# Gated memory attention with a GEGLU layer on one core: a third buffer for projected pairs, and the last chunk's side work put elsewhere

## The chip, the core and the metric

The kernel runs on one core of a Trainium2 chip. A core has five engines that work side by side: TensorE (matrix products), VectorE, ScalarE, GpSimd, and SyncE, which issues the transfers (DMAs). The metric is the device time of one launch in microseconds, the median of several runs.

## What is computed

The input x has 2,048 rows of 576 numbers. Two branches work on it, and a gate for each row mixes their results. Cut to what matters:

```python
g = sigmoid((x * gate_w).sum(-1, keepdims=True))
a = attention_with_memory(x, wq, wk, wv, wo, beta)
b = (gelu(x @ w_gate) * (x @ w_up)) @ w_down          # 576 -> 4608 -> 576
return g * a + (1 - g) * b

# attention_with_memory: 32 heads of 18 columns, 4 chunks of 512 rows
for s in range(4):
    qs, ks, vs = q[:, :, s], k[:, :, s], v[:, :, s]
    a_dot = softmax(qs @ ks.T * scale + mask) @ vs     # within the chunk
    a_mem = (phi(qs) @ M) / (phi(qs) @ z + 1e-6)       # from the chunks before
    outs.append(sigmoid(beta) * a_mem + (1 - sigmoid(beta)) * a_dot)
    M = M + phi(ks).T @ vs
    z = z + phi(ks).sum(over rows)
# phi(t) = t + 1 where t > 0, else exp(t)
```

## The kernel before, in words

**Pairs.** Numbers are kept as pairs of float16 tiles, a high word and a low word: ScalarE rounds to the high word, VectorE or GpSimd subtracts it from the float32 value to get the low word. Products take both words and add up in float32.

**Projections.** x is worked off in four chunks `s` of 512 rows. In a chunk after the first, TensorE begins with four row blocks `q`. Each makes the values of its 128 rows in two halves (`vrows`, L307 to L310, in the two banks `dn`), which VectorE turns into pairs (`put_rows`, `vstage`, L488) and a DMA stores. A half needs the bank that the vstage of an earlier half frees. Beside them stand the memory steps of the chunk before: `key_rows` (L548 to L551), `memorize` (L563) and `recall` (L520). Then come nine projections `j`, one for each column block of the queries and keys (`project`, L297 and L300). `put_columns` turns the result of one into a pair: ScalarE writes the high word (L453) into a tile `stage` and an exponential `expm` (L458), VectorE the low word (L465) and its part of phi (L463), GpSimd the rest of phi (L464), and SyncE issues the store `qk<-stage`. The tile `stage` has two buffers, so the pair after next waits for the store of this one.

Side work is put by hand into the row blocks (`beside_rows`) and the projections (`beside_products`): loading and splitting the next chunk of x, `rescale(c)` (L165: it brings two chunks to one scale, with one VectorE operation over 4,608 columns, L170), the sums of the parts of x that the later layer wants (`form_sums`: a subtraction L344, a high word on ScalarE L345, a low word on VectorE; `last_sum`: a subtraction on GpSimd L352 and words, the low word at L355), and for the first weights of that layer the sums of squares (`squares`, L80), the scales (`scales`, `scales_out`), their application on GpSimd (`scale_g`, L247) and their splitting into pairs (`high_g` on ScalarE, `low_g` on GpSimd L278, `sums_g` on GpSimd L267 to L270).

**The later layer and the attention.** After the fourth chunk a loop of 72 steps `v` runs over 36 blocks `f` of 128 hidden columns and the two halves `p` of the rows; v = 2f + p. A step makes the products of a block of `w_gate` and `w_up` with two chunks at once, seven products of parts and sums of parts in place of eight. They go to three banks, V, X (bank G) and Y (bank U):

```python
V, X, Y = bank("V"), bank("G"), bank("U")
product(V, f, S3, t, 8, 10, True); rest(V, ...)   # first
dve.tensor_copy(g1, V)                            # L1078
product(X, f, A11, x1, 0, 4, True); dve.tensor_copy(Y, X)   # L1082
product(V, f, A22, x2_, 0, 4); rest(V, ...)       # third; waits for L1078
...
product(Y, f, S1, t, 0, 2); dve.tensor_tensor(g1, Y, g1, OP.add)   # L1110
product(Y, f, S4, x2_, 2, 6); rest(Y, ...)        # last; waits for L1110
hidden(f, e, Y, g1)                               # L964, L968, L969
```

The products are at L984 and L991. From step 2 on, the attention of a head stands between them.

**Order.** The instructions of TensorE, VectorE, ScalarE and GpSimd run in the order in which the code issues them. The order on SyncE's queue is set by a scheduler from the whole program. A few operations of `put_columns` are issued later, by `finish_later()`. `zo` is the scale of the result, four lines at the end of the projections (L792 to L795), eight small operations once its helper is counted.

## Time and profile before

| | |
|---|---|
| median of 3 runs | 1689.53 us (1688.03 to 1690.39) |
| the profiled execution, its own time | 1691.98 us |
| its span in the profile | 1690.3 us |
| mean granted TensorE clock in it | 0.993 of full speed |
| busy: TensorE, VectorE, GpSimd, ScalarE | 97%, 75%, 68%, 64% of the span |

The span is what the profile sees of one execution; the rest of its own time lies around it. Times in rows of the profile count from the start of the span. A row of the timeline is start, duration, engine, line and operation, what is written and read, how many instructions (x12), and in brackets the idle time before it with what ended it: `[4.62 <-DVE vstage L488]` is 4.62 us of idleness that ended with VectorE's vstage. A row of waits is engine, tile and line, what it waited for, then the total, the count and the longest. A row of the stretches is start and end, length, TensorE's busy time with its count, the granted clock, the busy share of the DMA engines and the GB/s. A row of groups ends in count, busy time, mean ns and idle time before. Of the chain of waits a row is start, duration, engine and line.

In this profile the first chunk begins within the first 30 us; the row blocks of the second, third and fourth chunk begin near 65, 124 and 187 us, the loop of 72 steps at 254.7 us.

### The profile page before, as it was taken

What the parts mean: (1) busy time and instruction counts of PE and PEld (TensorE: products, weight loads), DVE (VectorE), ACT (ScalarE), POOL (GpSimd) and SP (SyncE); (2) the same over time, 40 slices, a digit from 0 to 9 for tenths busy, and PEclk for the clock granted to TensorE, in tenths of its full rate; (3) what the DMA queues carried; (4) which work ended last, traced back from release to release, by engine and by line L of the source; (5) the groups of instructions that cost most, each with busy time, mean ns of one, the idle gap of its engine ahead of it and who ended that gap; (6) DMA issues with size and microseconds to landing.
All of it is one profiled execution on the core that took longest, in us unless ns stands there. A gap on an engine that the chain in (4) does not pass through costs nothing.

```text
span 1690.3 us, 31950 instructions
## 1 busy us (share of the span) xinstructions
PE 1638.8 (97%) x11884; PEld 987.6 (58%) x11884; DVE 1266.0 (75%) x3154; ACT 1083.6 (64%) x1770; POOL 1146.5 (68%) x1057
## 2 busy tenths in 40 slices
PE   8899898899999999999999999999999999999999
PEld 4556654455655556655556555565555555565577
DVE  5556686688788888888788777888887887876543
ACT  6565344777767777777777777767777677762200
POOL 2231445887878888887869697887878797875300
PEclk9999999999999999999999999999999999999999
DMA  6522332556666465656566564747466565635351
GB/s 222 193 98 89 127 109 71 113 109 124 119 130 131 104 128 109 124 112 125 113 141 121 114 126 103 143 100 137 110 131 128 117 129 107 131 70 119 85 120 64
DMA packets 462348, 200.54 MB, mean 119 GB/s; under 512 B 421232, under 2 KB 431728, under 8 KB 461680
## 3 DMA queue, kind: packets, MB, share of 16 engines
q1 hardware_dynamic: 462192, 198.50, 52.7%
q8 instruction: 93, 1.52, 0.4%
q14 instruction: 63, 0.52, 0.1%
HBM read 82.60 MB, written 27.26 MB: 65 GB/s over the span
## 4 chain that ended last, share of the span: by engine, by line
PE 68%; DVE 16%; ACT 7%; POOL 4%; issue 3%; DMA 2%; DVEq 0%; ACTq 0%; SPq 0%; POOLq 0%
PE dn L942 17%; PE U L984 13%; PE V L984 7%; PE G L984 7%; PE pv L896 3%; DVE pf L854 3%; PE st L307 3%; PE st L848 3%; PE V L991 2%; DVE acc L950 2%; DVE junk L80 2%; PE dn L307 2%; PE U L991 2%; DMA qk<-stage 1%; POOL hh L969 1%
## 5 line engine op out<-in xcount | busy, mean ns | idle before, releaser
L942 PE MATMUL dn<-paird,hh 128*128 128x288 f16 x3402 | 488.4, 286 | 4.9 <-DVE acc L950 4.0
L984 PEld LDWEIGHTS <-pairg 128*128 128x128 f16 x3024 | 290.6, 98 | 298.2 <-issue 27.6
L877 POOL TENSOR_TENSOR ph<-pf,ph 128x512 f16<-128x512 f32 (+1 forms) x256 | 358.8, 1402 | 96.3 <-ACT ph L876 59.0
L942 PEld LDWEIGHTS <-hh 128*128 128x128 f16 x3456 | 337.1, 98 | 144.2 <-issue 7.9
L950 DVE SCALAR_TENSOR_TENSOR acc<-dn,ev,acc 128x288 f32<-128x288 f32 x535 | 268.0, 512 | 51.1 <-PE dn L942 48.7
L867 ACT ACTIVATE pf<-pf,mb,esc 128x512 f32<-128x512 f32 (+3 forms) x512 | 292.9, 642 | 3.0
L854 DVE CUSTOM_DVE_ANT_0 pf<-st,mask 128x512 f32<-128x512 f32 (+3 forms) x512 | 229.2, 485 | 75.6 <-PE st L848 72.5
L969 POOL TENSOR_TENSOR hh<-gl,hh 128x512 f16<-128x512 f32 x144 | 173.3, 1204 | 141.3 <-ACT hh L968 141.2
L984 PE MATMUL U<-xt,pairg 128*128 128x512 f16 x864 | 211.5, 381 | 4.8 <-DVE gl L1093 3.9
L984 PE MATMUL G<-x,pairg 128*128 128x512 f16 x864 | 210.0, 379 | 0.5 <-DVE stage L465 0.5
L278 POOL TENSOR_TENSOR pairg<-raw,pairg 128x512 f16<-128x512 f32 (+2 forms) x144 | 179.2, 1266 | 36.9 <-ACT pairg L274 36.9
L876 ACT ACTIVATE ph<-pf 128x512 f16<-128x512 f32 (+1 forms) x256 | 184.3, 720 | 0.0
L974 ACT ACTIVATE gl<-gl,sc 128x512 f32<-128x512 f32 x144 | 103.6, 720 | 94.1 <-DVE gl L1110 52.4
L864 ACT ACTIVATE mb<-mx,esc 128x4 f32<-128x4 f32 x128 | 37.4, 292 | 191.0 <-DVE mx L854 190.8
L968 ACT ACTIVATE hh<-gl 128x512 f16<-128x512 f32 x144 | 89.6, 622 | 86.5 <-DVE gl L964 86.5
L247 POOL TENSOR_SCALAR raw<-raw,sc 128x640 f32<-128x640 f32 x72 | 137.1, 1916 | 0.0
L1093 DVE COPY gl<-U 128x512 f32<-128x512 f32 x72 | 49.8, 692 | 108.8 <-POOL hh L969 55.1
L984 PE MATMUL V<-x,pairg 128*128 128x512 f16 x432 | 105.3, 380 | 10.9 <-DVE gl L1078 10.9
L848 PE MATMUL st<-kt,qt 72*128 72x512 f16 (+3 forms) x512 | 111.5, 299 | 0.6 <-DVE mx L854 0.6
L984 PE MATMUL U<-x,pairg 128*128 128x512 f16 x432 | 105.3, 379 | 2.5 <-DVE gl L1110 2.3
L984 PE MATMUL V<-xt,pairg 128*128 128x512 f16 x432 | 105.0, 379 | 0.0
L80 DVE CUSTOM_DVE_ANT_0 junk<-raw 128x640 bf16<-128x640 f32 x72 | 96.5, 1340 | 0.1
(249 smaller groups left out, 2530.6 us busy)
## 6 DMA issues: line engine op xcount, KB each, us to landing
raw<-in_wgu_dram SPq DMA_DIRECT2D x36, 640.0 KB
rawd<-in_wd_dram SPq DMA_DIRECT2D x36, 288.0 KB
qk<-stage SPq DMA_DIRECT2D x36, 256.0 KB
qt<-qk SPq DMA_DIRECT2D x128, 72.0 KB
kt<-qk SPq DMA_DIRECT2D x128, 72.0 KB
vp<-vstage SPq DMA_DIRECT2D x16, 296.0 KB
vt<-vp SPq DMA_DIRECT2D x16, 296.0 KB
orow<-oa SPq DMA_DIRECT2D x16, 288.0 KB
```

The lines of the kernel that those rows point to most:

```text
L80: dve.tensor_tensor_reduce(junk[:, : r.shape[1]], r, r, 1.0, 1e-30, OP.mult, OP.add, o)
L247: pool.tensor_scalar(r, r, scl[f // 2][0][:, 0:1], None, OP.mult)
L278: pool.tensor_tensor(spot(f, *p, 1), raw_g[f][:, p[0] : p[1]], spot(f, *p, 0), OP.subtract)
L848: pe.matmul(o[:, off : off + n], q[:, e * L + qi * P : e * L + (qi + 1) * P], kt[:, e * L : e * L + n], start=True, stop=True)
L854: dve.tensor_tensor_reduce(prob[a][:, COL[qi] : COL[qi + 1]], o[:, off : off + n], mask[:, L - n :], 1.0, -3e38, OP.add, OP.max, mx[a][:, ...
L867: act.activation(r, r, AF.Exp, bias=b[:, qi : qi + 1], scale=esc[:, 0, c : c + 1])
L876: act.activation(h[:, 0, cols], p[:, cols], AF.Copy)
L877: pool.tensor_tensor(h[:, 1, cols], p[:, cols], h[:, 0, cols], OP.subtract)
L942: pe.matmul(o[:, :NH], hh[:, a, q * P : (q + 1) * P], w[:, b, n * NH : (n + 1) * NH], start=i == 0, stop=i == 5)
L950: dve.scalar_tensor_tensor(av, o[:, :NH], ev, av, OP.mult, OP.add)
L969: pool.tensor_tensor(hh[:, 1], t, hh[:, 0], OP.subtract)
L984: pe.matmul(o, w[:, i, (a + k) * P : (a + k + 1) * P], x[:, b + k], start=start and k == 0 and i == 0 and b == h, stop=k == 1 and i == 1, ...
```

## The change

- `stage` gets three buffers in place of two.
- `form_sums` can be called for its subtraction alone (half -1) and for its high word alone (half 2). For the second pair of chunks the four subtractions move from the fourth chunk's projections j = 2 to 5 into its row blocks 0 to 3; high and low words follow in projections 1 to 5.
- `rescale` is cut in two: its small operations stay in row block 0, the large one (`rescale_words`, L170 before) moves to row block 2 for the fourth chunk. For the second chunk both stay together.
- The first weights' squares, scales, scaling and first splitting move up by a row block each; `sums_g` and the last sum `last_sum(1, 0)` come in projection 0.
- The load of the rest of x for the second pair moves from the fourth chunk's projection 1 to the third chunk's projection 3.
- A step's first product becomes a function, `first_product(v)`. Steps 0 and 2 call it for steps 1 and 3 ahead of their own last product.
- In step 0, `last_sum(1, 1)` moves from behind the second product to the end of the step. The scale `zo` moves to the end of step 1, as `scale_result()`.

```diff
     def rescale(c):
...
-        v = cst.tile([P, 1], F32, name="xr", tag="xr", bufs=2)
+        v = rescales[c] = cst.tile([P, 1], F32, name="xr", tag="xr", bufs=2)
         dve.tensor_scalar(v, xsc[:, b], xis[:, a], None, OP.mult)
-        dve.tensor_scalar(flat(x16[c]), flat(x16[c]), v, None, OP.mult)
         for t in (x2, xsc, xis):
             dve.tensor_copy(t[:, a], t[:, b])
+
+    def rescale_words(c):
+        dve.tensor_scalar(flat(x16[c]), flat(x16[c]), rescales.pop(c), None, OP.mult)
...
-        if half == 0:
+        if half <= 0:
             dve.tensor_tensor(r[o], r[a], r[b], OP.subtract)
+        if half == 0 or half == 2:
             act.activation(hi, r[o], AF.Copy, scale=sc)
-        else:
+        if half == 1:
             dve.scalar_tensor_tensor(lo, r[o][h], sc[h], hi[h], OP.mult, OP.subtract)
...
-            st = pp.tile([P, 2, L], F16, name="stage", bufs=2)
+            st = pp.tile([P, 2, L], F16, name="stage", bufs=3)
...
                 if s == 1 and q == 2:
                     rescale(0)
+                    rescale_words(0)
...
                 if s == 3:
+                    form_sums(1, q, -1)
                     if q == 0:
                         rescale(2)
-                    if q == 1:
                         for f, i in ((0, 0), (0, 1), (1, 0), (1, 1)):
                             squares(0, f, i)
-                    if q == 2:
+                    if q == 1:
                         scales(0)
                         scales_out(0)
+                        scale_g(0)
+                        squares(1, 2, 0)
+                    if q == 2:
+                        rescale_words(2)
                     if q == 3:
-                        scale_g(0)
+                        high_g(0, 0)
+                        low_g(0, 0)
+                        squares(1, 2, 1)
...
                     if j == 3:
                         load_sums(1)
+                        load_rest(1)
...
                 if s == 3:
                     if j == 0:
-                        high_g(0, 0)
-                        low_g(0, 0)
+                        sums_g(0)
+                        last_sum(1, 0)
                     if j == 1:
-                        sums_g(0)
-                    if j == 2:
                         high_g(0, 1)
-                    if j == 3:
                         low_g(0, 1)
                     if j == 4:
                         load_g(3)
-                    if 3 <= j < 7:
-                        form_sums(1, j - 3, 1)
+                    if 1 <= j < 5:
+                        form_sums(1, j - 1, 2)
                     if 2 <= j < 6:
-                        form_sums(1, j - 2, 0)
-                    if j in (6, 7):
-                        squares(1, 2, j - 6)
-                    if j == 7:
-                        last_sum(1, 0)
+                        form_sums(1, j - 2, 1)
...
+        def first_product(v):
+            f, p = divmod(v, 2)
+            V = bank("V")
+            product(V, f, S3, xt[p], 8, 10, True)
+            rest(V, f, G4, x16[2 * p + 1], 8)
+            return V
...
-            V, X, Y = bank("V"), bank("G"), bank("U")
-            product(V, f, S3, t, 8, 10, True)
-            rest(V, f, G4, x2_, 8)
+            V = ahead.pop(v) if v in ahead else first_product(v)
+            X, Y = bank("G"), bank("U")
...
             dve.tensor_copy(Y, X)
-            if v == 0:
-                last_sum(1, 1)
...
             some(fb - 1, early[3:])
+            if not fb and not p:
+                ahead[v + 1] = first_product(v + 1)
             hidden(f, c, X, g0)
...
             if v == 0:
+                last_sum(1, 1)
                 load_v(0)
+            if v == 1:
+                scale_result()
```

More of the change, by code (lines that the diff above doesn't have):

```diff
@@ L163, in low_x @@
             dve.scalar_tensor_tensor(t[64:, 8], r[64:, :L], xsc[64:, c : c + 1], t[64:, 8], OP.mult, OP.subtract)
+    rescales = {}
     def rescale(c):
         a, b = slice(c, c + 1), slice(c + 1, c + 2)
-        v = cst.tile([P, 1], F32, name="xr", tag="xr", bufs=2)
+        v = rescales[c] = cst.tile([P, 1], F32, name="xr", tag="xr", bufs=2)
         dve.tensor_scalar(v, xsc[:, b], xis[:, a], None, OP.mult)
-        dve.tensor_scalar(flat(x16[c]), flat(x16[c]), v, None, OP.mult)
         for t in (x2, xsc, xis):
             dve.tensor_copy(t[:, a], t[:, b])
+    def rescale_words(c):
+        dve.tensor_scalar(flat(x16[c]), flat(x16[c]), rescales.pop(c), None, OP.mult)
     raw_g, pair_g, raw_d, pair_d, scl = {}, {}, {}, {}, {}
@@ L333, in form_sums @@
     def form_sums(p, i, half):
-        r, t, sc = sums_x[p], kept["xt"][p], xsc[:, 2 * p : 2 * p + 1]
+        r, sc = sums_x[p], xsc[:, 2 * p : 2 * p + 1]
+        t = kept["xt"][p] if half >= 0 else None
         if i < 3:
             k, o, a, b = ((0, (1, 1), (1, 2), (1, 1)), (2, (1, 2), (2, 2), (1, 2)), (1, (2, 2), (2, 2), (1, 1)))[i]
-            hi, lo = (flat(t[:, 4 * k + j : 4 * k + j + 2]) for j in (0, 2))
             h = slice(0, P)
+            if t is not None:
+                hi, lo = (flat(t[:, 4 * k + j : 4 * k + j + 2]) for j in (0, 2))
         else:
             o, a, b = 0, 0, 1
-            hi, lo = t[:, 12], t[64:, 12]
             h = slice(64, P)
-        if half == 0:
+            if t is not None:
+                hi, lo = t[:, 12], t[64:, 12]
+        if half <= 0:
             dve.tensor_tensor(r[o], r[a], r[b], OP.subtract)
+        if half == 0 or half == 2:
             act.activation(hi, r[o], AF.Copy, scale=sc)
-        else:
+        if half == 1:
             dve.scalar_tensor_tensor(lo, r[o][h], sc[h], hi[h], OP.mult, OP.subtract)
@@ L779 @@
                         xt.append(mp2.tile([P, 13, L], F16, name="xt1", bufs=1))
-                        load_rest(1)
                     beside_products(s, j)
@@ L790, with scale_result @@
             finish_later()
-            zo = wts.tile([P, 2], F32, name="zo", tag="zo", bufs=1)
-            dve.tensor_reduce(zo[:, 1:2], x2, AX.X, OP.max)
-            dve.tensor_tensor(zo[:, 0:1], wz[:, 1:2], zo[:, 1:2], OP.mult)
-            scale_of(3, zo[:, 0:1])
+    def scale_result():
+        zo = wts.tile([P, 2], F32, name="zo", tag="zo", bufs=1)
+        dve.tensor_reduce(zo[:, 1:2], x2, AX.X, OP.max)
+        dve.tensor_tensor(zo[:, 0:1], wz[:, 1:2], zo[:, 1:2], OP.mult)
+        scale_of(3, zo[:, 0:1])
     with tc.tile_pool(name="keep", bufs=2, side="right", reuse_waits="tile") as kp, ExitStack() as tail:
@@ L1040, in down_squares @@
                 squares(fb + 2, n0 + 2, 2)
+        ahead = {}
+        def first_product(v):
[4 more added lines that the diff above has]
+            return V
         def step(v):
```

## The prediction

> **What bounds the kernel now.** First the page: how much of the span TensorE is busy.

> ```profile
> span 1690.3 us, 31950 instructions
> PE 1638.8 (97%) x11884; PEld 987.6 (58%) x11884; DVE 1266.0 (75%) x3154; ACT 1083.6 (64%) x1770; POOL 1146.5 (68%) x1057
> ```

> TensorE is idle for 51.5 us in all (1690.3 less 1638.8). The change touches only the projections and the first four pair steps, which lie before 320 us, so I next asked for TensorE's waits there, and for ScalarE's (total, count, longest):

> ```profile
> PE dn L307 <- DVE vstage L488: 8.6, 3, 4.6
> PE U L984 <- DVE gl L1093: 3.9, 2, 2.5
> PE dn L520 <- POOL phi L464: 2.1, 1, 2.1
> PE dn L309 <- DVE x L163: 2.0, 1, 2.0
> ...
> ACT stage L453 <- DMA qk<-stage: 22.7, 10, 3.7
> ```

> TensorE waits for VectorE at the head of each chunk (L488), for GpSimd's last phi once, and for copies in the pair steps. ScalarE waits ten times for the store of a pair whose buffer it wants. Third, the stretches around these waits: start and end, length, TensorE busy, granted clock.

> ```profile
> 62.00:74.00 12.00, 7.37 (x39) 0.72 0.70 240
> 184.00:194.00 10.00, 5.38 (x30) 0.83 0.39 144
> 237.00:248.00 11.00, 8.89 (x34) 0.69 0.17 60
> ```

> The clock column matters: all three stretches ran partly at half clock. Between 237 and 248 a mean of 0.69 loses 3.4 us (0.31 x 11) beside the idle time. The chain of waits says what stands behind the vstage waits (start, length):

> ```profile
> 60.81 4.50 DMA qk<-stage
> ...
> 118.12 3.18 DMA qk<-stage
> 123.97 1.92 DVE acc L344
> ...
> 179.22 4.11 DMA qk<-stage
> 186.21 2.26 DVE x L170
> ```

> At each chunk's end the chain is: store of a pair, ScalarE's next pair, VectorE's half of it, a step beside the rows (L344 or L170), vstage, TensorE.

> **The change part by part.**

> *a, third buffer, first to second chunk.*

> ```profile
> 60.96 0.60 ACT L453 ACTIVATE stage<-st 128x512 f16<-128x512 f32 x1 [2.51 <-DMA qk<-stage]
> 70.53 2.92 PE L307 MATMUL dn<-wv,x 128*128 128x288 f16 x12 [2.07 <-DVE vstage L488]
> 126.31 1.63 PE L307 MATMUL dn<-wv,x 128*128 128x288 f16 x12 [1.87 <-DVE vstage L488]
> 189.06 2.90 PE L307 MATMUL dn<-wv,x 128*128 128x288 f16 x12 [4.62 <-DVE vstage L488]
> 205.62 1.64 PE L307 MATMUL dn<-wv,x 128*128 128x288 f16 x12
> ```

> The pair at 60.96 waits 2.51 for the store two projections back; with three buffers it asks for the one three back. TensorE's idle time in 62 to 74 is 4.63 (12.00 less 7.37), all behind VectorE work that the late pairs push on. The twelve matmuls at 70.53 took 2.92 at half clock, against 1.63 in the full-clock row at 126.31: 1.3 lost, and I estimate 0.9 more on those between the gaps. Upper bound of the gain: 4.6 + 2.2 = 6.8. It is not all to be had. In the changed order of SP's queue both 1,024 KB loads of x stand ahead of the fourth pair's store, where one of them now stands behind it; a store beside such a load took 4.50 (chain, 60.81). So I expect the last pair still to wait, and vstage to end some 2 after TensorE wants it, instead of the 4.5 that it is late now. Lower bound: half of the upper, 3.5. I take 5.0, nearer to the middle.

> *b, second to third chunk.* The wait is 1.87 at full clock. VectorE's pair comes earlier by the store's wait (3.18 in the chain is issue to landing; about 2 of it is wait), so the whole gap goes. Gain 1.8; bounds 1.2 and 1.9. What is late next is nothing: L344 still runs before vstage, but 2 earlier.

> *c, third to fourth chunk.* Here the change fills what the buffer frees.

> ```profile
> 183.43 0.60 ACT L453 ACTIVATE stage<-G 128x512 f16<-128x512 f32 x1 [3.08 <-DMA qk<-stage]
> 191.91 0.82 DVE L80 CUSTOM_DVE_ANT_0 junk<-raw 128x640 bf16<-128x640 f32 x1
> 227.42 2.17 DVE L344 TENSOR_TENSOR acc<-acc 128x1024 f32<-128x1024 f32 x1
> L344 DVE TENSOR_TENSOR acc<-acc 128x1024 f32<-128x1024 f32 (+1 forms) x4 | 5.3, 1317 | 0.0
> ```

> ScalarE's wait of 3.08 goes, and up to 1.3 more since its earlier pairs are early too. Out of VectorE's queue ahead of vstage goes L170 (2.26). Into it come one subtraction (1.3 by the group's mean, 2.17 at 227.42 beside GpSimd) and four sums of squares at 0.82 each, 3.3: 4.6 to 5.5. So vstage moves by -3.1 to -4.4 for ScalarE and by 2.3 to 3.2 for VectorE: from -2.2 to +0.1, which is what TensorE gains here. I take 1.0. Over 3 us of the gap stay, and its half clock with them. The rest of the moved work lies beside the rows: at the second row block 1.3 to 2.2 for the subtraction and 0.82 for squares, at the third the subtraction and L170, 3.6 to 4.4. TensorE's next row block there asks only for the vstage before these, and the one after that comes some 8 us later (189.06 to 205.62 are two row blocks), so they cost nothing unless GpSimd's scalings, now beside them, stretch them to more than that. SP's load of the x tail was already issued early, and stays.

> *d, recall at the end.*

> ```profile
> 224.26 2.75 PE L297 MATMUL U<-x,wp 128*128 128x512 f16 x12
> 238.52 1.26 POOL L464 TENSOR_TENSOR phi<-phi,expm 128x512 f32<-128x512 f32 x1 [2.52 <-ACT xt L345]
> 239.84 0.44 PE L520 MATMUL dn<-bd,phi 64*128 64x76 f32 x2 [2.11 <-POOL phi L464]
> 243.33 4.69 PE L297 MATMUL U<-x,wp 128*128 128x512 f16 x12
> ```

> The recall waits 2.11 for the phi at 238.52, and then the clock halves: twelve matmuls take 4.69, not 2.75. The four subtractions, 5.3 us by the group row above, leave VectorE's queue ahead of that phi; one sum of squares, 0.8, enters. The phi comes some 4.5 earlier, wanted 2.1 earlier: 2.4 to spare. GpSimd does more before the first phi (low words, sums, and the last subtraction), but begins it a row block sooner. So wait and half clock go: 2.1 + 3.4 = 5.5. Lower bound 2.1, if another gap halves the clock anyway.

> [...] If the half clock had another cause and stayed, part d would be 2.1 and the sum below 3.4 smaller.

> *e, first product of the next pair.*

> ```profile
> 259.21 1.28 DVE L355 SCALAR_TENSOR_TENSOR x<-acc,xsc,x 128x1024 f16<-128x1024 f32 x1
> 265.39 1.46 PE L984 MATMUL U<-x,pairg 128*128 128x512 f16 x6 [0.78 <-DVE gl L1110]
> 267.38 0.75 DVE L964 SCALAR_TENSOR_TENSOR gl<-U,sc,gl 128x512 f32<-128x512 f32 x1
> 268.05 1.03 DVE L80 CUSTOM_DVE_ANT_0 junk<-rawd 128x576 bf16<-128x576 f32 x1
> 268.84 1.46 PE L984 MATMUL G<-x,pairg 128*128 128x512 f16 x6
> 269.11 0.69 DVE L1078 COPY gl<-V 128x512 f32<-128x512 f32 x1
> 270.13 1.46 PE L984 MATMUL V<-x,pairg 128*128 128x512 f16 x6
> 298.76 0.69 DVE L1078 COPY gl<-V 128x512 f32<-128x512 f32 x1 [3.14 <-POOL hh L969]
> ```

> The eight matmuls of step 1's first product fill the gap of 0.78 before 265.39. They take about 1.7: the six at 268.84 last 1.3 up to 270.13, and two more, narrower in count, a third of that. But the third product (270.13) may start only when VectorE has copied V, and that copy stays behind step 0's last L964, its squares, and now also the last words of x16 (L355), which move in front of it. From the end of that step's fourth product, VectorE does 0.75 + 1.03 + 1.28 + 0.69 = 3.8; TensorE has one product, 1.3, to cover it (before: also the first product, 3.0 in all, against 2.5). The fourth product of step 0, from 265.39, ended about 267.1 (270.13 less 1.3 and 1.7); it now ends 0.9 later (1.7 less 0.78), and the third of step 1 starts 3.8 and some 0.2 of handing over behind that, at about 272.1 instead of 270.13: 2.0 lost, a wait of 2.5 to 2.9, bounds 1.5 and 2.7. The three gaps quoted here of 2 us and over were followed by half clock, that of 1.87 at 126.31 was not, so I add one half-clock stretch, 1.5 (0 to 1.7): part e costs 3.5.

> At step 3 the copy of V waits for GpSimd's hh (298.76), as it does now; the product pulled ahead there only lengthens TensorE's wait in front of it. GpSimd sets the pace there, so this is worth nothing. I let none of step 1's loss be caught up by it, for GpSimd's work comes late by as much. The eight small operations for zo move from step 0, where nothing waited for them, to the end of step 1, in front of a copy: 0.3 at most, hidden by the same GpSimd stretch. In step 0 the wait for the last pair stays.

> **Sum.** -5.0 - 1.8 - 1.0 - 5.5 + 3.5 = -9.8. From 316 us on TensorE is busy nearly without a break in both, so the shift reaches the end. The profiled execution took 1691.98 (span 1690.3 and 1.7 around it): 1682.2. It lies 2.45 above the median of the three runs, 1689.53, for which I forecast 1679.7.

> **Rivals.**

> *R1, no half clock at step 1.* The wait of 2.9 there may be too short to cost the clock; part e is then 2.0. Sum -11.3: 1678.2. Against it: the gaps of 2.07 and 2.11 were followed by half clock. For it: 1.87 stayed at full clock. [...]

> *R2, the queue and not the buffers.* With three buffers ScalarE asks for older stores, but the loads in front hold these as long. Part a falls to 2.0 and c to -0.1 (a loss). For it: the 4.50 at 60.81. Against it: the store at 179.22 landed 4.11 after its issue with little ahead of it, and the third buffer gives 3.0 more. Sum -2.0 - 1.8 + 0.1 - 5.5 + 3.5 = -5.7: 1683.8.

> *R3, slower: the copy of V behind slowed words.* Squares beside GpSimd's subtraction once took 2.88:

> ```profile
> 240.35 2.88 DVE L80 CUSTOM_DVE_ANT_0 junk<-raw 128x640 bf16<-128x640 f32 x1
> ```

> That is 3.5 times 0.82. As one mechanism: whatever VectorE does beside GpSimd goes at that pace, and the change puts more of it there. In step 1 both the squares (2.6) and the words (4.5) stand beside GpSimd's four sums: VectorE then needs 0.75 + 2.6 + 4.5 + 0.69 = 8.5 from the end of the fourth product, the third of step 1 starts some 6.4 late, and with two half-clock stretches each at steps 1 and 3 (four of 1.7) part e is 13.2. At the fourth chunk's third row block the subtraction (4.6) and L170 (7.9) stand beside GpSimd's scalings: 12.5 in a row block of 8, 4.5 late, and 1.5 of half clock, 6.0. Sum -13.3 for a to d, +13.2, +6.0: +5.9, 1695.4. It decides where such slowing costs 13.3 in all; by 16.7 the kernel is slower by more than a measurement can miss. Against it: at 268.05 squares beside the same sums took 1.03, and the subtraction at 227.42 was 1.6 times the mean and not 3.5.

> **How the numbers follow.** Forecast 0.52, R1 0.15, R2 0.18, R3 0.15 (it needs a slowing seen once to hold everywhere, but it stands for the one engine the change loads at two places). The best ends of the parts (6.8, 1.9, 2.2, 5.5, cost 1.5) give -14.9, their worst (3.5, 1.2, -0.1, 2.1, cost 4.4) -2.3: 1674.6 to 1687.2. Rounded outward at the top towards R3, inward below, the range is 1675.0 to 1688.0; what it leaves out is R3 but for its mild end, and a sliver below. A measurement here can tell about 0.2%, 3.4 us. Faster by more: forecast and R1 but for 0.07 at their worst bounds (0.60), R2 three quarters (0.13): 0.73. Within: those 0.07, R2's rest 0.05, R3's mild end 0.03: 0.15. Slower: 0.12 of R3.

> **What would show it.** ScalarE's waits for stores fall from 22.7 to under 6. No wait at L488 near 126; about 2 near 66 and over 3 near 187. No wait at the recall, and full clock after it. The 0.78 in step 0 is gone and a wait of 2.5 to 3 for the copy of V stands in step 1. Wrong would be: a recall that still waits (GpSimd's queue), row blocks of the fourth chunk over 8.5 us, or waits at step 1 above 5.

## The result, and the profile after

The changed kernel takes 1679.63 us (median of 6, 1678.79 to 1680.26) against 1689.67 for the kernel before (median of 6, 1688.03 to 1691.43): a ratio of 0.9941, 95% interval 0.9928 to 0.9954. That is 10.0 us less; 9.8 were forecast. The profiled execution took 1679.60, its span is 1677.9.

First the head of the page: TensorE's idle time is now 45.7 us (1677.9 less 1632.2), 51.5 before. That is 5.8 of the 12.4 us by which the spans differ; the other 6.6 is busy time (1638.8 before, 1632.2 now) of the same 11,884 matmuls, of which fewer ran at half clock: the granted clock was 0.50 for 23.9 us in the kernel before (6.83 from 66.37 and from 240.45, 3.41 from 189.25, 308.71 and 1561.41) and for 6.8 now (3.41 from 255.87 and from 303.66), the ends of the span left out.

```profile
span 1677.9 us, 31940 instructions
PE 1632.2 (97%) x11884; PEld 984.0 (59%) x11884; DVE 1268.2 (76%) x3154; ACT 1084.0 (65%) x1770; POOL 1144.9 (68%) x1057
```

Then TensorE's waits in the first 320 us, and ScalarE's for stores (total, count, longest):

```profile
PE V L995 <- DVE gl L1097: 4.4, 2, 3.0
PE dn L311 <- DVE vstage L497: 4.3, 2, 3.4
...
PE dn L953 <- POOL paird L294: 1.9, 1, 1.9
...
ACT stage L462 <- DMA qk<-stage: 1.7, 1, 1.7
```

ScalarE waits once for a store, 1.7 us, where it waited ten times, 22.7. The three waits for vstage have become two (8.6 to 4.3), the recall's wait is gone, and the copy of V (L1097 now) costs 4.4 in place of 1.8. The rows behind these:

```profile
65.36 1.63 PE L311 MATMUL dn<-wv,x 128*128 128x288 f16 x12 [0.85 <-DVE vstage L497]
179.22 1.63 PE L311 MATMUL dn<-wv,x 128*128 128x288 f16 x12 [3.45 <-DVE vstage L497]
255.49 2.40 PE L995 MATMUL V<-x,pairg 128*128 128x512 f16 x6 [3.02 <-DVE gl L1097]
```

TensorE does the same products in nearly the same order in both kernels, so the difference of start times of the same product says what has been gained up to there. Six products in the kernel before, then the same six in the changed one: a projection of the first chunk, one of each later chunk, the first product of the loop, and the one of step 1 behind the copy of V.

```profile
35.08 2.75 PE L297 MATMUL st<-x,wp 128*128 128x512 f16 x12 [0.71 <-DVE gate L490]
89.44 2.75 PE L297 MATMUL G<-x,wp 128*128 128x512 f16 x12
149.27 2.75 PE L297 MATMUL G<-x,wp 128*128 128x512 f16 x12
213.78 2.75 PE L297 MATMUL G<-x,wp 128*128 128x512 f16 x12
254.70 1.47 PE L984 MATMUL V<-xt,pairg 128*128 128x512 f16 x6
273.29 1.46 PE L984 MATMUL G<-x,pairg 128*128 128x512 f16 x6
```

```profile
35.46 2.75 PE L301 MATMUL st<-x,wp 128*128 128x512 f16 x12 [0.71 <-DVE gate L499]
82.98 2.75 PE L301 MATMUL G<-x,wp 128*128 128x512 f16 x12
140.78 2.75 PE L301 MATMUL G<-x,wp 128*128 128x512 f16 x12
202.34 2.75 PE L301 MATMUL G<-x,wp 128*128 128x512 f16 x12
237.83 1.47 PE L995 MATMUL V<-xt,pairg 128*128 128x512 f16 x6
260.35 1.46 PE L995 MATMUL G<-x,pairg 128*128 128x512 f16 x6
```

The differences are +0.4, -6.5, -8.5, -11.4, -16.9 and -12.9; at the end of the span -12.4. The steps between them are the parts:

| part | forecast | bounds | these two executions |
|---|---|---|---|
| a, first to second chunk | -5.0 | -3.5 to -6.8 | -6.8 |
| b, second to third | -1.8 | -1.2 to -1.9 | -2.0 |
| c, third to fourth | -1.0 | -2.2 to +0.1 | -3.0 |
| d, recall | -5.5 | -2.1 to -5.5 | -5.4 |
| e, step 1 | +3.5 | +1.5 to +4.4 | +3.9 |
| start, and all after step 1 | 0 | | +0.9 |
| sum | -9.8 | | -12.4 |

The spans differ by 12.4, the medians by 10.0. Where the 2.4 went is told below, with the clock.

### The profile page after: what moved, and what is told of

Same layout as the page of the kernel before. It is cut to its first block, busy times and chain, and to the rows that moved or that the text cites. A ratio compares the mean times of both kernels' runs of the same rounds, so it can differ in the third digit from the quotient of the medians.

```text
span 1677.9 us, 31940 instructions
## 1 busy us (share of the span) xinstructions
PE 1632.2 (97%) x11884; PEld 984.0 (59%) x11884; DVE 1268.2 (76%) x3154; ACT 1084.0 (65%) x1770; POOL 1144.9 (68%) x1057
## 4 chain that ended last, share of the span: by engine, by line
PE 72%; DVE 15%; ACT 6%; POOL 3%; issue 2%; DMA 1%; SPq 0%; DVEq 0%; ACTq 0%; POOLq 0%
PE dn L953 17%; PE U L995 14%; PE V L995 7%; PE G L995 7%; DVE pf L865 3%; PE pv L907 3%; PE st L311 3%; PE st L859 3%; DVE acc L961 3%; DVE junk L80 2%; PE V L1002 2%; PE st L301 2%; PE dn L311 2%; PE U L1002 2%; PE G L301 2%
## 5 line engine op out<-in xcount | busy, mean ns | idle before, releaser
L995 PEld LDWEIGHTS <-pairg 128*128 128x128 f16 x3024 | 290.3, 98 | 299.8 <-issue 25.1
L1110 DVE COPY gl<-U 128x512 f32<-128x512 f32 x72 | 49.8, 692 | 110.4 <-PE U L995 56.1
L1002 PEld LDWEIGHTS <-pairg 128*128 128x128 f16 x576 | 56.4, 98 | 68.4 <-issue 0.6
```

The costliest lines, as they stand in the source:

```text
L995: pe.matmul(o, w[:, i, (a + k) * P : (a + k + 1) * P], x[:, b + k], start=start and k == 0 and i == 0 and b == h, stop=k == 1 and i == 1, ...
L1002: pe.matmul(o, w[:, i, a * P : (a + 1) * P], x[:, b], start=False, stop=i == 1, skip_group_check=True)
```

## The experiments

Each run stands beside the kernel before, measured with it: 1689.65 us with runs 1 to 4, 1690.52 with 5 to 7, 1690.61 with 8. So runs of different groups are compared by their ratio to it; that of the changed kernel is 0.9941 (0.9928 to 0.9954).

**1. The buffer alone, in the kernel before.**

```diff
-            st = pp.tile([P, 2, L], F16, name="stage", bufs=2)
+            st = pp.tile([P, 2, L], F16, name="stage", bufs=3)
```

> The kernel before with the third stage buffer and nothing else. Parts theory (each part worth what TensorE's matched matmuls show: first chunk end -6.8, second -2.0, third up to the whole wait of 4.62 with its half clock, -4.4 to -6.0, since nothing is put into the place): wait for vstage at the fourth chunk under 1, recall still waits 2.1 with half clock behind it, total -13 to -15: 1675 to 1677. Rival (the buffer pays only where the side work is moved with it; vstage stays behind the rescaling): first two chunks gain 6.8 and 2.0 at most and the third under 1: 1680 to 1682. Rival (the gain of the changed kernel is mostly where half clock happened to fall): under -5.

1674.67 us (1673.68 to 1677.3), ratio 0.9910 (0.9897 to 0.9924): one number in one line gains 15.0 us, more than the whole change. TensorE's waits from 60 to 260 us in this run:

```profile
PE dn L520 <- POOL phi L464: 2.1, 1, 2.1
PE dn L307 <- DVE vstage L488: 1.4, 2, 0.9
PE U L984 <- DVE gl L1110: 0.8, 1, 0.8
```

The waits for vstage shrink to 1.4 in sum (0.85 at the first chunk's end, 0.56 at the third's), with the 2.28 us of rescaling still ahead of the fourth chunk's vstage. The recall waits 2.1 as before, and 6.8 us at half clock follow it (225.79 to 232.60, granted clock 0.50). The parts theory holds; the two rivals are out.

**2. Everything but the buffer.**

```diff
-            st = pp.tile([P, 2, L], F16, name="stage", bufs=3)
+            st = pp.tile([P, 2, L], F16, name="stage", bufs=2)
```

> The changed kernel with two stage buffers as before. Parts theory: the first two chunk ends as before (0), the fourth chunk's vstage later than before by the work put ahead of it (2.3 to 3.2, a wait of 7 or so in place of 4.62), recall -5.4, step 1 +3.8: total +0.7 to +1.6, 1690 to 1691.5; ten waits of ScalarE for stores, 22 us. Rival (the moves pay without the buffer): -3 or more, 1686.5 or less.

1692.05 us (1690.02 to 1694.25), ratio 1.0013 (1.0004 to 1.0022). The moves by themselves cost 2.4 us, somewhat more than worked out. ScalarE waits for stores about as often as in the kernel before (in the first 320 us 12 times, 24.1 us, against 10 and 22.7). From 60 to 260 us:

```profile
ACT stage L462 <- DMA qk<-stage: 19.3, 9, 4.2
PE dn L311 <- DVE vstage L497: 10.8, 3, 7.0
```

The longest wait for vstage is the forecast 7: the work put ahead of the fourth chunk's vstage and the late pair add up. So of the four kernels (neither change 1689.65, the moves alone 1692.05, the buffer alone 1674.67, both 1679.63) the moves cost 2.4 without the buffer and 5.0 with it.

**3. The loop's first steps in the old order.** No product ahead, `last_sum(1, 1)` and `zo` where they were.

```diff
-            if not fb and not p:
-                ahead[v + 1] = first_product(v + 1)
...
             dve.tensor_copy(Y, X)
+            if v == 0:
+                last_sum(1, 1)
```

> The changed kernel with the loop's first steps ordered as before: no product ahead, the last words of x and zo at their old places. Parts theory: step 1's wait of 3.02 and the half clock behind it go, the 0.78 in step 0 returns: -3.8 against the changed kernel, 1675.9. Rival (GpSimd sets the pace in steps 1 to 4, so TensorE's gain at step 1 is waited off again by step 4): within 1 of 1679.6.

1674.78 us (1673.66 to 1676.75), ratio 0.9912 (0.9898 to 0.9925): 4.9 less than the changed kernel. GpSimd's pace in steps 1 to 4 hides none of it.

**4. Only the last words of x back.**

```diff
             dve.tensor_copy(Y, X)
+            if v == 0:
+                last_sum(1, 1)
...
             if v == 0:
-                last_sum(1, 1)
                 load_v(0)
```

> The changed kernel with last_sum(1, 1) alone back behind step 0's second product; the products stay ahead. Parts theory: 1.73 of words leave VectorE's queue ahead of the copy of V, the wait of 3.02 falls to about 1.3, which is too short for the half clock: -1.7 - 1.5 = -3.3, 1676.3. If the words were not the cause (the squares or the copy's other inputs hold it), the wait stays above 2.5 and the time at 1679.6. Rival as in the run before: the gain waited off by step 4.

1676.03 us (1674.49 to 1677.33), ratio 0.9918 (0.9904 to 0.9931): 3.6 of the 4.9. The product behind the copy of V now waits 1.36 and runs at full clock, its six matmuls in 1.46, where the changed kernel took 2.40:

```profile
254.46 1.46 PE L995 MATMUL V<-x,pairg 128*128 128x512 f16 x6 [1.36 <-DVE gl L1097]
```

**5. The fourth chunk's first vstage ahead of the squares.**

```diff
                         rescale(2)
+                        finish_later()
                         for f, i in ((0, 0), (0, 1), (1, 0), (1, 1)):
                             squares(0, f, i)
```

> The changed kernel with the fourth chunk's first vstage issued ahead of the four sums of squares (the first subtraction stays ahead of it). If the side work in VectorE's queue makes the wait of 3.45, it falls to 0.4 or so, with up to 0.8 in new short waits behind it: -2.3 to -3.0, 1676.6 to 1677.3. If GpSimd's or ScalarE's part of vstage held it, the wait stays above 3 and the time at 1679.6.

1679.94 us (1678.91 to 1680.95), ratio 0.9935 (0.9922 to 0.9949): 1.0 by the ratios, inside the noise, where 2.3 to 3.0 were expected; a miss. The wait for vstage is gone, and another stands behind the next product, with half clock after it (twelve matmuls of the recall at 182.60 take 3.36, those at 172.94 took 1.76; the mean clock from 176 to 192 is 0.79, which makes 6.7 us at half clock):

```profile
181.33 0.24 PE L557 MATMUL st<-ident,phi 64*128 64x64 f32 x1 [2.83 <-DVE mo L548]
```

TensorE's next work but one wants the bank `st`, which the recall filled and VectorE empties into `mo`. That emptying stands behind the squares too; the last of the four squares, and the emptying:

```profile
179.08 0.82 DVE L80 CUSTOM_DVE_ANT_0 junk<-raw 128x640 bf16<-128x640 f32 x1
180.73 0.82 DVE L548 TENSOR_TENSOR mo<-st,rden 128x288 f32<-128x288 f32 x2
```

I had worked out the two dn banks and not the st banks.

**6. Three of the four subtractions back.** The first stays in row block 0, so that the wait there is not touched; GpSimd's last subtraction goes back with the three.

```diff
                 if s == 3:
-                    form_sums(1, q, -1)
                     if q == 0:
+                        form_sums(1, 0, -1)
...
-                    if 1 <= j < 5:
-                        form_sums(1, j - 1, 2)
+                    if 3 <= j < 7:
+                        form_sums(1, j - 3, 1)
                     if 2 <= j < 6:
-                        form_sums(1, j - 2, 1)
+                        form_sums(1, j - 2, 0 if j > 2 else 2)
+                    if j == 7:
+                        last_sum(1, 0)
```

> The changed kernel with three of the four subtractions and GpSimd's last subtraction back in the projections (the first stays in row block 0, so that the wait there is left alone). If VectorE's subtractions made the recall wait, phi comes 3.7 later with 2.4 to spare: a wait of 1.3 to 2.2, and 1.7 to 3.4 of half clock if 2.0 or more of it falls into one window: +1.3 to +5.5, 1681 to 1685. If it was other work (squares, low words of the weights), no wait at the recall and 1679.6.

1679.43 us (1678.66 to 1680.89), ratio 0.9936 (0.9924 to 0.9949): the same as the changed kernel. TensorE's waits from 215 to 245 us:

```profile
PE G L996 <- DVE stage L474: 0.5, 1, 0.5
PE dn L529 <- POOL phi L473: 0.3, 1, 0.3
```

With three subtractions back the phi is late again, but by 0.3 only, so that the half clock expected behind 2.0 us of waiting in one window (a length of 3.41 us, last section) was not put to the test. So the three subtractions use up what there was to spare, and do not by themselves make the old wait of 2.1. The rest then comes from what else left the projections ahead of that phi, the first subtraction and the weights' words. The weights' last squares it is not, for in the kernel before they stand behind that phi in VectorE's queue (the first of them at 240.35):

```profile
237.62 0.74 DVE L463 TENSOR_SCALAR phi<-G,al 128x512 f32<-128x512 f32 x1
```

Which of the two makes it, no run tells apart.

**7. Both losses taken out, as I then saw them.** The edits of 3 and 5 together.

> The third buffer and the moves in the row blocks and projections, with the loop's first steps in the old order and the fourth chunk's first vstage ahead of the squares: both losses of the changed kernel taken out. Parts theory: 1674.8 less 2.3 to 3.0 for the wait, and less 1.7 where half clock followed it: 1670.1 to 1672.5. If TensorE's time in front of the loop is waited off in it (GpSimd's pace), 1674 or more.

1676.69 us (1676.37 to 1677.0), ratio 0.9919 (0.9905 to 0.9932): not below the run with the old order alone (0.9912), and outside the 1670.1 to 1672.5 of the parts theory. It has the same 2.8 of waiting for `mo` as run 5, and twelve matmuls of the recall behind it take the 3.36 that they take there; in run 3 they take 2.28, in the changed kernel 1.84:

```profile
182.23 3.36 PE L529 MATMUL st<-bd,phi 128*128 128x152 f32 x12
```

The loss is there before the loop: the product U behind the wait of 0.78 in step 0 starts at 251.38, in run 3 at 249.83. So it is not GpSimd's pace in the loop that took the gain.

**8. The squares behind the recall's rows.** With the old order in the loop; in the fourth chunk:

```diff
                     if q == 0:
                         rescale(2)
+                    if q == 1:
                         for f, i in ((0, 0), (0, 1), (1, 0), (1, 1)):
                             squares(0, f, i)
-                    if q == 1:
+                    if q == 2:
                         scales(0)
                         scales_out(0)
                         scale_g(0)
-                        squares(1, 2, 0)
-                    if q == 2:
-                        rescale_words(2)
                     if q == 3:
-                        high_g(0, 0)
-                        low_g(0, 0)
-                        squares(1, 2, 1)
+                        rescale_words(2)
+                        squares(1, 2, 0)
...
                     if j == 0:
+                        high_g(0, 0)
+                        low_g(0, 0)
                         sums_g(0)
-                        last_sum(1, 0)
...
+                    if j == 6:
+                        squares(1, 2, 1)
+                    if j == 7:
+                        last_sum(1, 0)
```

> The third buffer, the subtractions in the row blocks and the weights' words in the first projections, with the loop's first steps in the old order; the four sums of squares back in row block 1 (behind the recall's own rows, not only behind vstage), the scales in row block 2, the large rescaling in row block 3. If VectorE's queue in the fourth chunk's first row block is the only cost left: waits there of under 1 (with the buffer alone and the rescaling of 2.28 ahead of vstage it was 0.56), none at the recall, so 3.0 less than with the old order in the loop alone, and 0 to 1.7 more where half clock followed: 1670 to 1672. Rival: the later scales bring GpSimd's low words late and the recall waits again, or TensorE's lead is waited off in the loop: 1674 or more.

1670.06 us (1669.23 to 1673.13), ratio 0.9876 (0.9859 to 0.9892): 20 us under the kernel before, and below the buffer alone (0.9897 at the lower bound of that). All of TensorE's waits from 60 to 260 us:

```profile
PE U L995 <- DVE gl L1129: 1.6, 2, 0.8
PE dn L311 <- DVE vstage L497: 0.9, 1, 0.9
PE G L995 <- DVE stage L474: 0.5, 1, 0.5
```

No wait in the fourth chunk's row blocks, none at the recall. This is the version to keep: the buffer, the recall's gain, and neither of the two costs.

## Why the prediction was right, and where it was not

**The total came out within 0.1 us, and two of its steps were wrong by far more than that.** Parts a and c were put 3.8 too small in sum; the step from one execution to the median took 2.4 of it away again, and part e with the two ends of the span 1.3. The direction and the rank of the parts were right; the exactness is chance.

**a.** "vstage to end some 2 after TensorE wants it" is the step that failed. The last pair does wait for a store, 1.7, as expected, but vstage is late by 0.85 (row at 65.36) and no half clock follows: the twelve matmuls take 1.63. The waits for x in the same stretch (L160 and L163 in the kernel before, 0.6 and 2.0) are gone too. The upper bound, 6.8, was the value. The order on SyncE's queue did change as forecast, two loads of x and then two stores, and it did so with the buffer alone. The changed kernel, then run 1:

```profile
47.27 1.08 SPq L328 DMA_DIRECT2D acc<-in_xs_dram  x2
51.01 2.46 SPq L475 DMA_DIRECT2D qk<-stage  x2
```

```profile
47.72 1.08 SPq L324 DMA_DIRECT2D acc<-in_xs_dram  x2
51.47 2.46 SPq L466 DMA_DIRECT2D qk<-stage  x2
```

In that order ScalarE waited 1.7 and 1.8 for stores, not 22.7, so the loads did not hold the older stores up: R2 is out. What the buffer would gain in the old order of the queue, no run shows.

**b.** As forecast: no wait is left.

**c.** The sum of moves was right: a wait of 3.45 where "over 3 us" was to stay. "And its half clock with them" was wrong in this execution: 1.63 in place of 2.90 for the twelve matmuls. Both terms came out as given: with the buffer alone the wait falls from 4.62 to 0.56 (run 1), by 4.1, and the work put ahead of vstage brings 2.9 of it back. The rest of the moved work in the row blocks makes no wait of TensorE there, as forecast.

**d.** The size was right in these two executions, 5.4. The reason, that the four subtractions leave the queue, was a part of it only (run 6).

**e.** The mechanism was right: the copy of V behind L964, squares and words, a wait of 3.02 where 2.5 to 2.9 was given, half clock behind it for 3.41 us (from 255.87), a loss of 1.7 where 1.5 was added. The copy ends at 255.44 and the product starts at 255.49, so the handing over put at 0.2 took 0.05. The words took 1.73 and the squares 1.20 instead of 1.28 and 1.03; they stand beside GpSimd's sums. Run 4 shows the words as the cause, run 3 the price of the whole part, 4.9 at the median.

**R1** asked for no half clock at step 1; it came here, yet in run 6 the products behind the same wait of 3.02 ran at full clock (six matmuls in 1.47, here 2.40; last section). **R3** did not come about: the squares at step 1 took 1.20, not 2.6, and the words 1.73, not 4.5:

```profile
251.97 1.20 DVE L80 CUSTOM_DVE_ANT_0 junk<-rawd 128x576 bf16<-128x576 f32 x1
253.10 1.73 DVE L364 SCALAR_TENSOR_TENSOR x<-acc,xsc,x 128x1024 f16<-128x1024 f32 x1
254.76 0.68 DVE L1097 COPY gl<-V 128x512 f32<-128x512 f32 x1
```

**From one execution to the median.** The profiled execution of the kernel before had a granted clock of 0.993; 24 of its 31 further runs (15, 9 and 7) had 0.994 or 0.995. In the mean over those 31 runs the time goes with the clock: 1688.8 in the six at 0.996, 1690.2 in the twelve at 0.995, 1690.8 in the twelve at 0.994, 1692.1 in the one at 0.993. A thousandth of the clock over 1690 us is 1.7 us, one stretch of 3.41 us at half clock. By these numbers, as an estimate, one or two of the half-clock stretches in that execution, which parts a, c and d booked as gains, are not there to be gained in the median run; which ones, no trace says. The forecast moved the whole sum over to the median.

## What to carry to other kernels

Make the cheap edit alone first: one more buffer gained 15 us, and the moves made to go with it cost 5 of these back. Side work on an engine that works in the order of issue, as VectorE did (in run 5 the emptying at 180.73 stands behind the square at 179.08), has to be placed behind every release that the busiest engine waits for, not only the one that shows in the profile: take one wait away, and ask which bank the next product wants, and what stands in front of its emptying. Where a profile shows half clock behind short gaps, count it as a gain only as often as other executions show it too.

## What the runs showed of the hardware

```profile
173.95:177.36 3.41, 1.82 (x14) 1.29 (x15) 3.34 (x10) 0.42 (x1) 0.44 (x3) 1.00 0.61 224
177.37:180.78 3.41, 1.56 (x13) 1.25 (x13) 3.27 (x12) 0.00 (x0) 0.00 (x0) 1.00 0.00 0
180.78:184.19 3.41, 3.41 (x27) 2.76 (x26) 3.38 (x13) 1.14 (x3) 0.97 (x2) 1.00 0.47 178
```

The kernel of run 3:

```profile
173.42:176.83 3.41, 2.11 (x16) 1.50 (x17) 3.37 (x9) 0.42 (x1) 0.72 (x3) 1.00 0.75 281
176.84:180.24 3.40, 1.26 (x11) 1.01 (x11) 3.25 (x11) 0.00 (x0) 0.00 (x0) 1.00 0.00 1
180.25:183.66 3.41, 3.41 (x16) 2.65 (x15) 2.63 (x10) 1.14 (x3) 0.00 (x0) 0.50 0.46 175
```

The same gap is split 1.6 and 1.9 in the one and 1.3 and 2.15 in the other, and only the second is followed by half clock. In run 4 it is split 2.0 and 1.5 (windows from 174.96 and 178.38) with none behind it; in run 6 the 2.2 in the window from 175.08 are followed by it. The wait of 3.02 at step 1 in the changed kernel, and in run 6:

```profile
252.46:255.87 3.41, 0.40 (x3) 0.21 (x3) 3.41 (x5) 0.26 (x1) 3.17 (x4) 1.00 0.44 117
255.87:259.28 3.41, 3.41 (x10) 1.21 (x8) 0.17 (x1) 0.00 (x0) 1.47 (x2) 0.50 0.13 36
```

```profile
253.58:257.00 3.42, 2.40 (x12) 0.88 (x9) 2.71 (x6) 1.37 (x2) 3.34 (x4) 1.00 0.49 123
257.00:260.41 3.41, 1.42 (x7) 0.70 (x8) 2.54 (x3) 0.00 (x0) 3.25 (x4) 1.00 0.30 86
260.42:263.82 3.40, 3.40 (x19) 1.69 (x17) 1.46 (x4) 0.02 (x1) 0.41 (x1) 1.00 0.09 21
```

It fell into one window (3.0 idle) in the first and into two (1.0 and 2.0) in the second, which kept its clock.

In the kernel before and the changed one, the windows at full clock with 1.85 us or more of idle time on TensorE, beside that of 3.0 (the ends of the span left out): those with 2.11 (from 237.03), 2.19 (1557.99), 2.54 (305.30) and 3.24 (185.83, all four in the kernel before) were followed by half clock. At 1.85 to 1.96 it went both ways: 1.96 (62.95, before) and 1.87 (300.25, changed) were followed by it, 1.87 (124.39, before), 1.85 (177.37, changed) and 1.90 (1546.11, changed) were not. Each of the seven stretches at half clock has one of these windows in front of it. Why a stretch lasts 3.41 or 6.83 no run shows: the one of 6.83 from 240.45 and the one of 3.41 from 189.25 both had no idle time in their first window, the one of 6.83 from 66.37 had 1.33.

So gaps of 3.0 and 3.5 us cost a half-clock stretch in some traces (3.02 in the changed kernel, 3.46 in run 3) and none in others (3.02 in run 6, 3.45 in the changed kernel). That this also makes a part of the spread of 4 us that one kernel shows from run to run (before, beside runs 5 to 7: 1687.58 to 1692.12) fits the clock means above; it was not shown run by run.
